# Feed-forward steps of 512 tokens by 128 inner units in place of 256 tokens by 256, in a fused attention and feed-forward kernel

## Chip, core and metric

The kernel runs on one core of one Trainium2 chip. The metric is the device time of one execution in microseconds (us). Besides plain executions there is one profiled execution with a trace of every engine: TensorE (PE, with its weight loads shown apart as PEld), VectorE (DVE), ScalarE (ACT), GpSimd (POOL), and SyncE (SP), which issues all DMAs here. Each engine works through its own queue strictly in order, and waits where an instruction's inputs or its buffer are not ready.

## What is computed

All data are float32; there are 4 batches, 8 heads, 768 positions, a head width of 64, and so 3072 tokens of width 512.

```python
# attention: a band of |i-j| < 16 in full, and 24 block summaries for the rest
k_sum = k.reshape(B, H, 24, 32, 64).max(axis=3)
v_sum = v.reshape(B, H, 24, 32, 64).mean(axis=3)
scores = concat([where(band, q @ k.T / 8, -1e9), q @ k_sum.T / 8 + log(32)])
a = softmax(scores)
x = (a @ concat([v, v_sum])).reshape(3072, 512)      # heads side by side
# feed-forward, w_in 512 x 2048, w_out 2048 x 512 (float64 in memory)
h = x @ w_in
g = h * tanh(softplus(h))                            # Mish
out = g @ w_out
```

## The kernel before

**Attention.** The 3072 tokens are 12 chunks of 256 (`NCH`, `CH`). A chunk is worked on in four units, one for each pair of heads (`HP`). A unit goes around all engines: `att_scores` (L240) does four score matmuls into one PSUM tile `sc` (L246; chunk 0 has smaller ones in L252 and L254), the mask and the row maximum on DVE (L261, four pairs of instructions), four exponentials on ACT (L266), the reciprocal of the sums on DVE (L269, L270), and the scaling on POOL (L271). `att_transpose` (L274) transposes on PE (`pt_ps`, L278) and copies on ACT (`pt`, L280). `att_values` (L283) multiplies by the values on PE (`x_ps`, L295); ACT rounds the result to `xh` (L296) and DVE takes the rest `xl` (L297). `sc`, `pt_ps` and `x_ps` share two PSUM buffers (`ps_a`; chunk 0 uses those of `ps_o`). The loads of a unit (`qk`, `vw`) have two buffers each.

**Precision.** Each feed-forward product is made of three matmuls, of a high and a low part: high by high, low by high, high by low.

**Weights.** 32 blocks of weights (16 of each matrix) come in as float64 and are turned into a high and a low part by `load_weight` (L107): per block four DVE instructions (L116, L117, L120, L122), two on ACT (L119, L124), one on POOL (L125). The loads go through three `stage` buffers, which the key and value summaries of batches 1 to 3 (`ks`, `vsum`) share.

**Feed-forward.** A step covers one chunk and 256 inner units. `ff_in` (L303) has 24 matmuls with 256 moving columns (L313) into `ph`, one PSUM bank of two (`ps_h`); `ff_act` (L317) is Mish on ACT (L321), the high part (L325, on ACT for chunks 0 and 1, else on DVE) and the low part on DVE (L326); `ff_out` (L329) has 12 matmuls with 512 columns (L340) into two banks `po`. There are 8 steps a chunk, 96 in all.

**Order.** The code before the main loop does chunk 0's attention and loads the first four weight blocks (L359). The main loop (L381) runs the steps of chunks 0 and 1 interleaved, and the others in order; `ff_out` follows two steps behind. The table `at` (L365 to L374) says at which step the parts of a unit are emitted, so that a chunk's four units are spread over the eight steps before it. Four, later two, weight blocks are loaded per step (L394). A scheduler then places the instructions on the engines' queues, so the emitted order is not quite the one that runs.

Of the kernel before, what the change touches and what calls it, by code (L numbers as in the profile page):

```python
# [55 lines left out]
def fused_kernel(ctx: ExitStack, tc: tile.TileContext, q0, qk, kt, v0, vw, vs, w_in, w_out, out):  # L56
# [49 lines left out]

    def load_weight(src, hi, lo, name):  # L107
        t = stage.tile([P, WP], I64, tag="stage", name=name)
        nc.sync.dma_start(t, src)
# [6 lines left out]
        nc.vector.tensor_scalar(out=x, in0=low, scalar1=29, scalar2=None, op0=ALU.logical_shift_right)  # L116
# [5 lines left out]
        nc.vector.scalar_tensor_tensor(out=u, in0=u, scalar=3, in1=x,  # L122
                                       op0=ALU.logical_shift_left, op1=ALU.bitwise_or)
        nc.scalar.copy(hi, f)  # L124
# [157 lines left out]

    def att_values(c, hp):  # L283
        u = units.pop((c, hp))
        if c not in xs:
            xs[c] = (xp.tile([P, HP, CH], F32R, tag="xh", name=f"xh{c}"),
                     xp.tile([P, HP, CH], F32R, tag="xl", name=f"xl{c}"))
        xh, xl = xs[c]
        ps = att_psum(c, f"x_ps{c}_{hp}")
        for s in range(NQ):  # L290
            for h in range(2):
                d = slice(h * D, (h + 1) * D)
# [2 lines left out]
                nc.tensor.matmul(x, u["v"][:, s, d], pt, start=True, stop=True)  # L295
# [7 lines left out]
    def ff_in(c, fp):  # L303
        i = c, fp
        xh, xl = xs[c]

        pool, tag = (ps_a, "a") if c == NCH - 1 and fp in (NP_ - 1, NP_ - 3) else (ps_h, "h")
        ph = pool.tile([P, 2, CH], F32, tag=tag, name=f"ph{c}_{fp}")
        for j in range(2):
            wh, wl = (weight(0, part, 2 * fp + j) for part in range(2))  # L310
            for cc in range(NCC):
                for n, (w, x) in enumerate(((wh, xh), (wh, xl), (wl, xh))):
                    nc.tensor.matmul(ph[:, j, :], w[:, cc * P:(cc + 1) * P], x[:, cc, :],  # L313
                                     start=(cc == 0 and n == 0), stop=(cc == NCC - 1 and n == 2))
        st[i] = {"h": ph.rearrange("p j t -> p (j t)")}

    def ff_act(c, fp):  # L317

        s = st[c, fp]
        g = ff.tile([P, 2 * CH], F32, tag="g", name=f"g{c}_{fp}", bufs=3)  # L320
        nc.scalar.activation(g, s["h"], AF.Mish)  # L321
        gh = ff.tile([P, 2 * CH], F32R, tag="gh", name=f"gh{c}_{fp}", bufs=3)
        gl = ff.tile([P, 2 * CH], F32R, tag="gl", name=f"gl{c}_{fp}", bufs=3)

        (nc.scalar.copy if c < 2 else nc.vector.tensor_copy)(gh, g)  # L325
        nc.vector.tensor_sub(gl, g, gh.bitcast(F32))  # L326
        s["g"] = (gh, gl)

    def ff_out(c, fp):  # L329
        i = c, fp  # L330
        gh, gl = st.pop(i)["g"]
        if fp == 0:
            po[c] = [ps_o.tile([P, DM], F32, tag="o", name=f"po{c}_{t}") for t in range(CH // P)]
        for t in range(CH // P):
            for j in range(2):
                fc = 2 * fp + j
                tok = slice(j * CH + t * P, j * CH + (t + 1) * P)
                wh, wl = (weight(1, part, fc) for part in range(2))
                for n, (g, w) in enumerate(((gh, wh), (gl, wh), (gh, wl))):
                    nc.tensor.matmul(po[c][t], g[:, tok], w,  # L340
                                     start=(fc == 0 and n == 0), stop=(fc == NFC - 1 and n == 2))
        if fp == NP_ - 1:
            for t in range(CH // P):
                o = ff.tile([P, DM], F32, tag="o", name=f"o{c}_{t}")
                nc.scalar.copy(o, po[c][t])
                nc.sync.dma_start(out[c * CH + t * P:c * CH + (t + 1) * P, :], o)
# [17 lines left out]
    start = 0  # L366
    for c in range(1, NCH):
        n = steps.index((c, 0)) - start
        for hp in range(HP):
            k = min(start + n - 3, start + n - 3 - 2 * (HP - 1 - hp) if c == 2 else start + n * hp // HP - 1)  # L370
            at.setdefault(max(k, 0), []).append((att_scores, c, hp))
            at.setdefault(max(k, 0) + 1, []).append((att_transpose, c, hp))
            at.setdefault(max(k, 0) + 2, []).append((att_values, c, hp))
        start += n  # L374
# [4 lines left out]

    loaded = HP + 1  # L380
    for i in range(len(steps) + 2):  # L381
        parts = at.get(i, ())
        now = [x for k, x in enumerate(steps) if turn(k, 0) == i]
        for x in now:
            ff_in(*x)
        for x in now:
            ff_act(*x)
# [56 lines left out]
```

## Time and profile before

| | us |
|---|---|
| median of 3 runs | 713.8 (709.15 to 714.37) |
| the profiled execution's own time | 712.24 |
| its span, from the first to the last instruction | 710.5 |
| PE busy | 672.8 (95%) |
| ACT busy | 354.2 (50%) |
| DVE busy | 301.1 (42%) |
| POOL busy | 111.5 (16%) |

Matmuls overlap, so PE's busy time says where PE has work, and not how fast it does it. Busy shares are averages over stages that differ: DVE is at 42% overall and close to full in the first quarter. A row of a timeline gives start, duration, engine, line, instruction, and in brackets how long the engine had been idle and what ended that. A row of the chain of waits gives start, duration and what was on the path that ended last. A row of a table of windows gives the stretch, its length, the busy time of each engine with its instructions in brackets, the clock granted to PE (1.00 is full), and the DMA engines' share and rate.

### The profile page before, as it was taken

How to read it: one execution, taken by the hardware profiler on the slowest of the kernel's cores; microseconds unless marked ns; L12 is line 12 of the kernel's file. 1: busy time of each engine (PE TensorE's matmuls, PEld its weight loads, DVE VectorE, ACT ScalarE, POOL GpSimd, SP SyncE). 2: the span in 40 equal slices, each digit the busy share in tenths (PEclk: the TensorE clock that was granted, in tenths of full speed). 3: DMA queues.
4: the chain of work that ended last, by engine and by line, in shares of the span. 5: the costliest groups of instructions: out<-in, count | busy, mean ns of one | idle time of the engine just before them, and what ended most of it. 6: DMA issues, size and time to landing. Idle time of an engine off the chain costs nothing.

```text
span 710.5 us, 12644 instructions
## 1 busy us (share of the span) xinstructions
PE 672.8 (95%) x4960; PEld 603.6 (85%) x4960; DVE 301.1 (42%) x872; ACT 354.2 (50%) x776; POOL 111.5 (16%) x151
## 2 busy tenths in 40 slices
PE   4978788799999999999999999999999999999998
PEld 3767677688898998998998998998998998998996
DVE  4899989952322334443223233222222322322211
ACT  2767755544556644644644644644644644644110
POOL 3454554301010010010100100100100100010000
PEclk9969899899999999999999999999999999999999
DMA  9876655772221323531311311311311311300000
GB/s 276 239 235 204 184 171 155 216 230 88 88 71 44 111 56 104 161 89 43 116 43 43 116 43 44 117 44 43 116 43 43 117 43 44 115 15 1 30 1 30
DMA packets 30683, 70.56 MB, mean 99 GB/s; under 512 B 4768, under 2 KB 9504, under 8 KB 30624
## 3 DMA queue, kind: packets, MB, share of 16 engines
q1 hardware_dynamic: 30624, 69.76, 32.2%
q8 instruction: 39, 0.64, 0.4%
q14 instruction: 20, 0.16, 0.1%
HBM read 61.15 MB, written 6.29 MB: 95 GB/s over the span
## 4 chain that ended last, share of the span: by engine, by line
PE 79%; DVE 11%; DMA 4%; issue 2%; ACT 2%; SPq 0%; POOL 0%; DVEq 0%; POOLq 0%
PE ph L313 34%; PE po L340 33%; PE sc L246 6%; PE x_ps L295 3%; DVE w_x L116 3%; PE pt_ps L278 2%; DVE w_x L117 2%; DVE w_f L122 2%; DMA ks<-kt 1%; DMA vsum<-vs 1%; DMA vw<-vw 1%; DVE w_f L120 1%; ACT pr L266 1%; DVE gl L326 1%; DVE vq L196 1%
## 5 line engine op out<-in xcount | busy, mean ns | idle before, releaser
L313 PE MATMUL ph<-xh,w_early_in_hi 128*128 128x256 f32 x480 | 138.7, 291 | 3.2 <-ACT w_early_in_hi L124 2.4
L313 PE MATMUL ph<-xh,w_early_in_lo 128*128 128x256 f32 x480 | 139.1, 291 | 2.2 <-POOL w_early_in_lo L125 2.2
L313 PE MATMUL ph<-xl,w_early_in_hi 128*128 128x256 f32 x480 | 138.9, 290 | 1.2 <-DVE xl L297 1.2
L325 DVE CAST gh<-g 128x512 fp32r<-128x512 f32 x80 | 34.3, 429 | 209.3 <-ACT g L321 196.6
L271 POOL TENSOR_TENSOR pr<-pr,rs 128x480 f32<-128x480 f32 x48 | 49.0, 1021 | 348.2 <-DVE rs L270 309.7
L313 PEld LDWEIGHTS ph<-xh,w_early_in_hi 128*128 128x128 f32 x480 | 93.9, 196 | 7.1 <-ACT w_early_in_hi L124 3.2
L313 PEld LDWEIGHTS ph<-xl,w_early_in_hi 128*128 128x128 f32 x480 | 93.8, 196 | 3.9 <-DVE xl L297 1.7
L313 PEld LDWEIGHTS ph<-xh,w_early_in_lo 128*128 128x128 f32 x480 | 93.9, 196 | 3.2 <-POOL w_early_in_lo L125 2.6
L340 PE MATMUL po<-w_early_out_hi,gh 128*128 128x512 f32 x240 | 94.3, 396 | 2.5 <-ACT gh L325 2.5
L340 PE MATMUL po<-w_early_out_hi,gl 128*128 128x512 f32 x240 | 95.6, 398 | 0.0
L340 PE MATMUL po<-w_early_out_lo,gh 128*128 128x512 f32 x240 | 95.0, 396 | 0.0
L321 ACT ACTIVATE g<-ph 128x512 f32<-128x512 f32 x96 | 57.4, 598 | 67.0 <-PE ph L313 66.5
L313 PE MATMUL ph<-xh,w_late_in_hi 128*128 128x256 f32 x288 | 82.5, 287 | 0.1
L313 PE MATMUL ph<-xh,w_late_in_lo 128*128 128x256 f32 x288 | 81.9, 284 | 0.1
L313 PE MATMUL ph<-xl,w_late_in_hi 128*128 128x256 f32 x288 | 81.1, 282 | 0.0
L266 ACT ACTIVATE pr<-pr,nm 128x120 f32<-128x120 f32 x192 | 73.7, 385 | 5.8 <-DVE nm L261 5.3
L321 ACT ACT_TABLE_LOAD x44 | 56.5, 1283 | 38.7 <-PE ph L313 38.3
L326 DVE TENSOR_TENSOR gl<-g,gh 128x512 fp32r<-128x512 f32 x96 | 70.7, 736 | 8.1 <-ACT gh L325 5.5
L296 ACT CAST xh<-x_ps 128x256 fp32r<-128x256 f32 x48 | 17.9, 372 | 100.7 <-PE x_ps L295 100.7
L280 ACT COPY pt<-pt_ps 120x512 f32<-120x512 f32 x48 | 28.1, 586 | 71.9 <-PE pt_ps L278 71.5
L266 ACT ACT_TABLE_LOAD x43 | 55.2, 1283 | 8.4 <-DVE nm L261 7.8
L340 PE MATMUL po<-w_late_out_hi,gl 128*128 128x512 f32 x144 | 56.7, 394 | 1.6 <-DVE gl L326 1.6
(75 smaller groups left out, 1149.9 us busy)
## 6 DMA issues: line engine op xcount, KB each, us to landing
qk<-qk SPq DMA_DIRECT2D x44, 496.0 KB
vw<-vw SPq DMA_DIRECT2D x48, 192.0 KB
w<-w_in SPq DMA_DIRECT2D x16, 512.0 KB
w<-w_out SPq DMA_DIRECT2D x16, 512.0 KB
ks<-kt SPq DMA_DIRECT2D x16, 384.0 KB
out<-o SPq DMA_DIRECT2D x24, 256.0 KB
vsum<-vs SPq DMA_DIRECT2D x12, 384.0 KB
vw<-vm SPq DMA_DIRECT2D x44, 48.0 KB
```

What stands on the lines that cost most here:

```text
L116: nc.vector.tensor_scalar(out=x, in0=low, scalar1=29, scalar2=None, op0=ALU.logical_shift_right)
L246: nc.tensor.matmul(ps[:, s * KA:(s + 1) * KA], u["qk"][:, s, 0:P], u["qk"][:, s, P:], start=True, stop=True)
L266: nc.scalar.activation(pr[:, s, :], pr[:, s, :], AF.Exp, scale=-1.0, bias=nm[:, s:s + 1], accum_out=sm[:, s:s + 1])
L271: nc.gpsimd.tensor_mul(pr, pr, rs.unsqueeze(2).broadcast_to([P, NQ, KA]))
L280: nc.scalar.copy(pt.rearrange("p s q -> p (s q)"), ps[:KA, :])
L295: nc.tensor.matmul(x, u["v"][:, s, d], pt, start=True, stop=True)
L296: nc.scalar.copy(xh[:, hp, :], ps[:, :CH])
L313: nc.tensor.matmul(ph[:, j, :], w[:, cc * P:(cc + 1) * P], x[:, cc, :], start=(cc == 0 and n == 0), stop=(cc == NCC - 1 and n == 2))
L321: nc.scalar.activation(g, s["h"], AF.Mish)
L325: (nc.scalar.copy if c < 2 else nc.vector.tensor_copy)(gh, g)
L326: nc.vector.tensor_sub(gl, g, gh.bitcast(F32))
L340: nc.tensor.matmul(po[c][t], g[:, tok], w, start=(fc == 0 and n == 0), stop=(fc == NFC - 1 and n == 2))
```

## The change

Two chunks form a group of 512 tokens (`CG`, `TG`, six groups `NG`). A step now covers one group and 128 inner units: `ff_in` has 12 matmuls of 512 columns, `ff_out` 12 as before, but into four `po` banks. There are 16 steps a group, and again 96. The attention of chunks 0 and 1 stands ahead of all steps, with six weight blocks among it; then each step loads two. The units of chunks 2 and 3 start at steps 6 to 13 of the first group; those of a later group at every second step of the group before. The steps run in plain order (`LEAD` and `AHEAD` are gone; so are the two last `ph` tiles in `ps_a`). `x` has two buffers of a group in place of three of a chunk. The tiles `f`, `x`, `a` (the Mish output) and `o` share one ring of six buffers. Of the four output copies of a group two go to DVE.

```diff
-NP_ = NFC // 2
+CG = 2
+TG = CG * CH
+NG = NCH // CG
-LEAD = 4
-AHEAD = 3
...
-    ff = ctx.enter_context(tc.tile_pool(name="ff", bufs=2))
+    ff = ctx.enter_context(tc.tile_pool(name="ff", bufs=6))
...
-        f = ff.tile([P, WP], F32, tag="f", name=f"{name}_f", bufs=3)
-        x = ff.tile([P, WP], U32, tag="x", name=f"{name}_x", bufs=2)
+        f = ff.tile([P, WP], F32, tag="t", name=f"{name}_f")
+        x = ff.tile([P, WP], F32, tag="t", name=f"{name}_x").bitcast(U32)
...
+    def ff_in(g, fc):
+        xh, xl = xs[g]
+        ph = ps_h.tile([P, TG], F32, tag="h", name=f"ph{g}_{fc}")
+        wh, wl = (weight(0, part, fc) for part in range(2))
+        for cc in range(NCC):
+            for n, (w, x) in enumerate(((wh, xh), (wh, xl), (wl, xh))):
+                nc.tensor.matmul(ph, w[:, cc * P:(cc + 1) * P], x[:, cc, :],
+                                 start=(cc == 0 and n == 0), stop=(cc == NCC - 1 and n == 2))
+        st[g, fc] = ph
...
+            if fc == NFC - 1:
+                o = ff.tile([P, DM], F32, tag="t", name=f"o{g}_{t}")
+                (nc.vector.tensor_copy if t % 2 else nc.scalar.copy)(o, po[g][t])
...
-    for what in "K0 K1 S0 W1 K2 V0 S1 W1 T0 K3 V1 S2 A0 T1 W1 V2 S3 A1 T2 V3 A2 T3 W1 L0 A3".split():
-        begins[what[0]](int(what[1:]))
+    begin_with("K0 K1 S0 K2 V0 S1 W1 T0 K3 V1 S2 A0 T1 V2 S3 W1 A1 T2 V3 A2 T3 l0 W1 A3")
     begin.close()
...
+    begin_with("l1 s0 W1 t0 s1 l2 a0 t1 s2 W1 l3 a1 t2 s3 W1 a2 t3 l4 a3")
...
+    for c, hp in todo[CG * HP:]:
+        g, half = divmod(c, CG)
+        u = half * HP + hp
+        k = NFC // 2 - 2 + u if g == 1 else (g - 1) * NFC + 2 * u - 1
...
-        load_weights(4 if i < LEAD else 2)
+        load_weights(2)
```

In the changed kernel the matmuls of `ff_in` are L310, Mish L317, the high and low part L321 and L322, the matmuls of `ff_out` L333; `x_ps` is L296, `xh` L297, `xl` L298. A number directly behind the letters of a name counts pairs of heads (`sc`, `pr`, `pt`, `x_ps`), steps (`ph`, `a`, `g`) or token blocks (`po`); `xh` and `xl` have none, and are whole chunks before, whole groups after. The last number is a running one.

The queue of PE where a chunk of the kernel before ends, around the value matmuls of the last unit of the next chunk (here the change from chunk 6 to 7 or one like it):

```order
L313 MATMUL ph_0_4047<-xh_3576,w_early_in_hi 128x256
L313 MATMUL ph_0_4047<-xl_3577,w_early_in_hi 128x256
L295 MATMUL x_ps_3_3998<-pt_3_3965,vw_3_3772 64x64 x8
L246 MATMUL sc_0_4009<-qk_0_3899 128x120 x4
L313 MATMUL ph_0_4047<-xh_3576,w_early_in_lo 128x256
L313 MATMUL ph_0_4047<-xh_3576,w_early_in_hi 128x256
L313 MATMUL ph_0_4047<-xl_3577,w_early_in_hi 128x256
L313 MATMUL ph_0_4047<-xh_3576,w_early_in_lo 128x256
L313 MATMUL ph_0_4047<-xh_3576,w_early_in_hi 128x256
L313 MATMUL ph_0_4047<-xl_3577,w_early_in_hi 128x256
L313 MATMUL ph_0_4047<-xh_3576,w_early_in_lo 128x256
L340 MATMUL po_0_3675<-w_late_out_hi,gh_6_3944 128x512
```

The same place in the changed kernel, where the second group ends. All the `ff_out` of that group stand ahead of these rows; behind them come the last six matmuls of `ph_0` and `ph_1`, and then the twelve of `ph_2`:

```order
L278 MATMUL pt_ps_2_2544<-ident,pr_2_2480 120x128 x4
L296 MATMUL x_ps_2_2570<-pt_2_2549,vw_2_2392 64x64 x8
L246 MATMUL sc_3_2581<-qk_3_2495 128x120 x4
L310 MATMUL ph_0_2747<-xh_1916,w_early_in_hi 128x512
L310 MATMUL ph_1_2785<-xh_1916,w_early_in_hi 128x512
L310 MATMUL ph_0_2747<-xl_1917,w_early_in_hi 128x512
L310 MATMUL ph_0_2747<-xh_1916,w_early_in_lo 128x512
L310 MATMUL ph_1_2785<-xl_1917,w_early_in_hi 128x512
L310 MATMUL ph_1_2785<-xh_1916,w_early_in_lo 128x512
L278 MATMUL pt_ps_3_2661<-ident,pr_3_2586 120x128 x4
L296 MATMUL x_ps_3_2687<-pt_3_2666,vw_3_2498 64x64 x8
L246 MATMUL sc_0_2698<-qk_0_2605 128x120 x4
```

Before, only the value part of the last unit and the scores of the next stand at the chunk's end, with `ff_in` and then 24 matmuls of `ff_out` behind them. Now the transposes of units 2 and 3, their value matmuls and two sets of scores follow one another there, with six matmuls of `ff_in` between the scores of unit 3 and its transposes, and none between a unit's transposes and its value matmuls.

The queue of ACT at that place in the changed kernel:

```order
L280 COPY pt_1_2443<-pt_ps_1_2438 120x512
L297 CAST xh_1916<-x_ps_1_2464 128x256
L266 ACT_TABLE_LOAD
L266 ACTIVATE pr_2_2480,sm_2_2486<-pr_2_2480,nm_2_2481 128x120 x4
L280 COPY pt_2_2549<-pt_ps_2_2544 120x512
L297 CAST xh_1916<-x_ps_2_2570 128x256
L266 ACTIVATE pr_3_2586,sm_3_2592<-pr_3_2586,nm_3_2587 128x120 x4
L280 COPY pt_3_2666<-pt_ps_3_2661 120x512
L297 CAST xh_1916<-x_ps_3_2687 128x256
L266 ACTIVATE pr_0_2703,sm_0_2709<-pr_0_2703,nm_0_2704 128x120 x4
L317 ACT_TABLE_LOAD
L317 ACTIVATE a_0_2760<-ph_0_2747 128x512
```

Before, a Mish stands between any two sets of exponentials; now three sets of exponentials stand in a row here, and the next group's first Mish is behind the third.

The queue of DVE in the first stage of the kernel before, while chunk 1's units 0 and 1 are at their maxima (`w_..` are instructions of weight blocks):

```order
L261 ISA pr_0_511,nm_0_512<-sc_0_506,base 128x120
L261 ISA nm_0_512 128x1
L116 TENSOR_SCALAR w_2_x<-w_2_580 128x512
L122 SCALAR_TENSOR_TENSOR w_3_f<-w_3_f,w_3_x 128x512
L120 TENSOR_SCALAR w_2_f<-w_2_f 128x512
L261 ISA pr_1_537,nm_1_538<-sc_1_532,base 128x120
```

And in the changed kernel the last block of the six that go with chunks 0 and 1, with chunk 1's first unit behind it:

```order
L117 SCALAR_TENSOR_TENSOR w_3_x<-w_3_627,w_3_x 128x512
L298 TENSOR_TENSOR xl_298<-x_ps_2_410,xh_297 128x256
L122 SCALAR_TENSOR_TENSOR w_3_f<-w_3_f,w_3_x 128x512
L298 TENSOR_TENSOR xl_298<-x_ps_3_445,xh_297 128x256
L261 ISA pr_0_475,nm_0_476<-sc_0_470,base 128x120
```

From there on DVE's queue holds only the parts of seven units (the four of chunk 1 and the first three of chunk 2), 73 rows in all, up to this place, where the other 26 weight blocks begin:

```order
L261 ISA pr_2_1173,nm_2_1174<-sc_2_1168,last 128x120
L261 ISA nm_2_1174 128x1
L116 TENSOR_SCALAR w_2_x<-w_2_692 128x512
L116 TENSOR_SCALAR w_4_x<-w_4_703 128x512
L117 SCALAR_TENSOR_TENSOR w_2_x<-w_2_692,w_2_x 128x512
```

Before, weight blocks and units alternate on DVE from the start; now there is a stretch of units alone, and the first step's Mish and the weights stand behind it.

More of the change, by code (lines that the diff above doesn't have):

```diff
@@ L130, in load_weights @@
         del weights[:n]
-    weights = [(w, 2 * fp + j) for fp in range(NP_) for w in range(2) for j in range(2)]
+    weights = [(0, 0)] + [(w, fc + 1 - w) for fc in range(NFC) for w in range(2) if fc + 1 - w < NFC]
     begin = ExitStack()
@@ L235, in att_psum @@
     def att_psum(c, name):
-        pool, tag = (ps_o, "o") if c == 0 else (ps_a, "a")
+        pool, tag = (ps_o, "o") if c < CG else (ps_a, "a")
         return pool.tile([P, 512], F32, tag=tag, name=name)
@@ L284, in att_values @@
         u = units.pop((c, hp))
[L285 to L288, printed above, removed]
+        g, half = divmod(c, CG)
+        if g not in xs:
+            xs[g] = (xp.tile([P, HP, TG], F32R, tag="xh", name=f"xh{g}"),
+                     xp.tile([P, HP, TG], F32R, tag="xl", name=f"xl{g}"))
+        xh, xl = (x[:, hp, half * CH:(half + 1) * CH] for x in xs[g])
         ps = att_psum(c, f"x_ps{c}_{hp}")
@@ L295, in att_values @@
                 nc.tensor.matmul(x, u["v"][:, s, d], pt, start=True, stop=True)
-        nc.scalar.copy(xh[:, hp, :], ps[:, :CH])
-        nc.vector.tensor_sub(xl[:, hp, :], ps[:, :CH], xh[:, hp, :].bitcast(F32))
+        nc.scalar.copy(xh, ps[:, :CH])
+        nc.vector.tensor_sub(xl, ps[:, :CH], xh.bitcast(F32))
     st = {}
     po = {}
[L303 to L346, printed above, removed]
@@ new lines, in ff_in, with ff_act @@
+    def ff_in(g, fc):
[7 more added lines that the diff above has]
+        st[g, fc] = ph
+    def ff_act(g, fc):
+        a = ff.tile([P, TG], F32, tag="t", name=f"a{g}_{fc}")
+        nc.scalar.activation(a, st[g, fc], AF.Mish)
+        ah = ff.tile([P, TG], F32R, tag="ah", name=f"ah{g}_{fc}", bufs=3)
+        al = ff.tile([P, TG], F32R, tag="al", name=f"al{g}_{fc}", bufs=3)
+        (nc.scalar.copy if g == 0 else nc.vector.tensor_copy)(ah, a)
+        nc.vector.tensor_sub(al, a, ah.bitcast(F32))
+        st[g, fc] = ah, al
@@ new lines, in ff_out @@
+    def ff_out(g, fc):
+        ah, al = st.pop((g, fc))
+        if fc == 0:
+            po[g] = [ps_o.tile([P, DM], F32, tag="o", name=f"po{g}_{t}") for t in range(TG // P)]
+        wh, wl = (weight(1, part, fc) for part in range(2))
+        for t in range(TG // P):
+            tok = slice(t * P, (t + 1) * P)
+            for n, (a, w) in enumerate(((ah, wh), (al, wh), (ah, wl))):
+                nc.tensor.matmul(po[g][t], a[:, tok], w,
+                                 start=(fc == 0 and n == 0), stop=(fc == NFC - 1 and n == 2))
+            if fc == NFC - 1:
+                o = ff.tile([P, DM], F32, tag="t", name=f"o{g}_{t}")
+                (nc.vector.tensor_copy if t % 2 else nc.scalar.copy)(o, po[g][t])
+                nc.sync.dma_start(out[g * TG + t * P:g * TG + (t + 1) * P, :], o)
@@ L349, in fused_kernel @@
     todo = [(c, hp) for c in range(NCH) for hp in range(HP)]
-    steps = [(c, i - c * LEAD) for i in range(NP_ + LEAD) for c in range(2) if 0 <= i - c * LEAD < NP_]
-    steps += [(c, fp) for c in range(2, NCH) for fp in range(NP_)]
+    steps = [(g, fc) for g in range(NG) for fc in range(NFC)]
     begins = {"K": lambda n: att_load_keys(0, n), "V": lambda n: att_load_values(0, n),
               "S": lambda n: att_scores(0, n), "T": lambda n: att_transpose(0, n),
-              "A": lambda n: att_values(0, n), "W": load_weights, "L": lambda n: att_load(1, n)}
@@ L359, in fused_kernel, with begin_with @@
-    for what in "K0 K1 S0 W1 K2 V0 S1 W1 T0 K3 V1 S2 A0 T1 W1 V2 S3 A1 T2 V3 A2 T3 W1 L0 A3".split():
-        begins[what[0]](int(what[1:]))
+              "A": lambda n: att_values(0, n), "W": load_weights, "l": lambda n: att_load(*todo[HP + n]),
+              "s": lambda n: att_scores(1, n), "t": lambda n: att_transpose(1, n),
+              "a": lambda n: att_values(1, n)}
+    def begin_with(parts):
+        for what in parts.split():
+            begins[what[0]](int(what[1:]))
+    begin_with("K0 K1 S0 K2 V0 S1 W1 T0 K3 V1 S2 A0 T1 V2 S3 W1 A1 T2 V3 A2 T3 l0 W1 A3")
@@ L361, in fused_kernel @@
     begin.close()
     late += weight_tiles(ctx.enter_context(tc.tile_pool(name="late", bufs=1)), "w_late", NFC - EARLY)
+    begin_with("l1 s0 W1 t0 s1 l2 a0 t1 s2 W1 l3 a1 t2 s3 W1 a2 t3 l4 a3")
     at = {}
[L366 to L374, printed above, removed]
@@ L376, in turn @@
-    def turn(k, lag):
-        return k + lag - (k >= len(steps) - AHEAD)
-    loaded = HP + 1
+    for c, hp in todo[CG * HP:]:
+        g, half = divmod(c, CG)
+        u = half * HP + hp
+        k = NFC // 2 - 2 + u if g == 1 else (g - 1) * NFC + 2 * u - 1
+        at.setdefault(k, []).append((att_scores, c, hp))
+        at.setdefault(k + 1, []).append((att_transpose, c, hp))
+        at.setdefault(k + 2, []).append((att_values, c, hp))
+    loaded = CG * HP + 1
     for i in range(len(steps) + 2):
@@ L382, in fused_kernel @@
         parts = at.get(i, ())
[L383 to L387, printed above, removed]
+        if i < len(steps):
+            ff_in(*steps[i])
+            ff_act(*steps[i])
         for f, c, hp in parts:
```

2 lines of the change are left out of this document (1 added, 1 removed).

## The prediction

> **What bounds the kernel now.** I read the profile's head and its table of windows first, to see where PE idles; then the chain of waits in the steady part, for what a step and a unit cost on PE; then the timelines of DVE, ACT and PE where the change rearranges work.
>
> ```profile
> span 710.5 us, 12644 instructions
> core 0: us, PE busy (x) PEld busy (x) DVE busy (x) ACT busy (x) POOL busy (x), PEclk, DMA share, GB/s
> 37.20:133.60 96.40, 81.59 (x534) 71.42 (x535) 93.80 (x182) 64.29 (x140) 46.94 (x38) 0.88 0.63 195
> 133.60:190.60 57.00, 50.03 (x338) 44.60 (x337) 26.72 (x67) 27.23 (x57) 6.49 (x8) 0.91 0.50 151
> 190.60:657.80 467.20, 467.20 (x3512) 423.06 (x3512) 147.38 (x540) 235.44 (x511) 43.25 (x68) 1.00 0.23 70
> ```
>
> Three stages with different limits. From 37.2 to 133.6, DVE is busy 93.8 of 96.4 us: it turns weights into high and low parts, and PE waits for them. Up to 190.6 PE catches up. Then PE never idles for 467.2 us, at full clock: there, time is what stands on PE's queue.
>
> ```profile
> 37.24 0.39 PE L313 MATMUL ph<-xh,w_early_in_hi 128*128 128x256 f32 x1 [1.13 <-ACT w_early_in_hi L124]
> 404.17 2.86 PE ph L313 x24
> 407.03 2.75 PE po L340 x12
> 411.10 0.44 PE pt_ps L278 x4
> 415.95 0.61 PE x_ps L295 x16
> 416.57 1.08 PE sc L246 x8
> 706.65 0.39 PE L340 MATMUL po<-w_late_out_lo,gh 128*128 128x512 f32 x1
> ```
>
> A 256-column matmul costs PE 2.86/24 = 0.119 us, a 512-column one 2.75/12 = 0.2296. A step is 5.61 us; a unit adds 0.44 + 0.61 + 1.08 = 2.13. From the first feed-forward matmul (37.24) to PE's end (707.04) are 669.8 us. The work in it is 2304 × 0.1192 + 1152 × 0.2296 + 44 units × 2.13 = 632.8; the other 37 us are waits and half clock, all before 190.6. The tail behind PE is 3.4 us. The profiled execution took 712.24, its span plus 1.7; the median, 713.8, is 0.2% above. I forecast in the span's frame and add 1.7.
>
> **The change part by part.** *Width.* Each two 256-column matmuls become one of 512. Nothing here shows an `ff_in` matmul of 512 columns; the `ff_out` ones have the same width and type, so I take 0.2296. The bounds are that and 2 × 0.1192. The gain is 1152 × (0.2384 − 0.2296) = 10.1 us; a step becomes 5.51.
>
> *The stretch of units alone.* Chunk 0's attention and the six blocks stay about where they were, so the stretch begins near 38.5. Then DVE's in-order queue has 73 rows of seven units and no weight row, and DVE is the engine that bounded this stage. How long does a unit take when nothing covers its chain?
>
> ```profile
> 402.07 1.15 PE L246 MATMUL sc<-qk 128*128 128x120 f32 x8
> 403.37 0.28 DVE L261 CUSTOM_DVE_ANT_0 pr<-sc,base 128x120 f32<-128x120 f32 x1 [0.35 <-PE sc L246]
> 403.88 0.40 ACT L266 ACTIVATE pr<-pr,nm 128x120 f32<-128x120 f32 x1
> 406.01 0.17 DVE L269 TENSOR_SCALAR rs<-sm 128x4 f32<-128x4 f32 x1 [1.74 <-ACT pr L266]
> 406.22 0.18 DVE L270 RECIPROCAL rs<-rs 128x4 f32<-128x4 f32 x1
> 407.34 0.99 POOL L271 TENSOR_TENSOR pr<-pr,rs 128x480 f32<-128x480 f32 x1
> 410.94 0.60 PE L278 MATMUL pt_ps<-ident,pr 128*120 128x128 f32 x4
> 411.57 0.59 ACT L280 COPY pt<-pt_ps 120x512 f32<-120x512 f32 x1 [2.57 <-PE pt_ps L278]
> 645.18 0.40 ACT L266 ACTIVATE pr<-pr,nm 128x120 f32<-128x120 f32 x1
> 646.62 0.19 ACT L266 ACTIVATION_READ_ACCUMULATOR pr<-pr,nm 128x1 f32 x1
> 647.21 1.28 ACT L321 ACT_TABLE_LOAD   x1 [0.41 <-PE ph L313]
> 648.51 0.60 ACT L321 ACTIVATE g<-ph 128x512 f32<-128x512 f32 x1
> ```
>
> From the scores to DVE 1.30 us, to ACT 0.51, four exponentials in a row 1.63 (645.18 to 646.81), the reciprocals 0.39, POOL 0.99, and about 0.2 for hand-offs: 5.0 us until the transposes can start. They take 0.44 before the next scores: 5.44 a unit if each waits for the last. Below, ACT alone needs 1.63 + 0.59 = 2.2. So seven units take 16 to 38 us. In PE's order, five score sets follow the transposes of the unit before or wait for a shared `ps_a` buffer, and two overlap with them: 5 × 5.44 = 27. PE is mostly idle there, and then its work takes longer:
>
> ```profile
> 40.95 1.90 PE L246 MATMUL sc<-qk 128*128 128x120 f32 x8
> ```
>
> 1.90 for the scores in place of 1.08, and the like for transposes: some 1.2 us a unit, 6 in all. I take **33**, near the upper bound. The 24 `ff_in` matmuls that stand among these rows lie in the waits.
>
> *The weights behind it.* 26 blocks are left.
>
> ```profile
> 103.75 1.51 DVE L116 TENSOR_SCALAR w_x<-w 128x512 uint32<-128x512 uint32 x1
> 109.71 1.51 DVE L116 TENSOR_SCALAR w_x<-w 128x512 uint32<-128x512 uint32 x1
> L116 DVE TENSOR_SCALAR w_x<-w x26: 392/1146/1526, 38.2 to 125.8; 128x512 uint32<-128x512 uint32 x26
> 131.07 0.27 DVE L261 CUSTOM_DVE_ANT_0 pr<-sc,base 128x120 f32<-128x120 f32 x1
> 131.87 0.68 DVE L326 TENSOR_TENSOR gl<-g,gh 128x512 fp32r<-128x512 f32 x1
> 133.60 0.67 DVE L122 SCALAR_TENSOR_TENSOR w_f<-w_f,w_x 128x512 uint32<-128x512 uint32 x1
> L326 DVE TENSOR_TENSOR gl<-g,gh 128x512 fp32r<-128x512 f32 x96 | 70.7, 736 | 8.1 <-ACT gh L325 5.5
> L172 DVE TENSOR_REDUCE km<-ks 128x24 f32<-128x768 f32 x16 | 15.1, 944 | 6.5 <-DMA ks<-kt 6.5
> L196 DVE TENSOR_REDUCE vq<-vsum 96x32 f32<-96x1024 f32 x12 | 14.6, 1212 | 10.3 <-DMA vsum<-vs 6.4 <-DMA vm<-vq 3.9
> ```
>
> Two blocks lie between 103.75 and 109.71: 2.98 us a block. Before, 26 blocks also came after 38.2, with units among them, and the last ended at 134.3. Now: 26 × 2.98 = 77.5; 14 low parts of the Mish output at 0.65 (0.736 less the overlap) = 9.1; three units at 1.6 (maxima 0.80, reciprocals 0.35, `xl` 0.42) = 4.8; five summaries of keys at 0.87 = 4.3, four of values at 1.25 = 5. Together 101 us: 38.5 + 33 + 101 = **172.5** for the last block, against 134.3. PE can't run ahead of it: 13 steps of 5.51 fit easily into 101 us.
>
> Behind the last block PE still has, up to the third step of the second group, 64 matmuls (14.7 us), attention pieces (7.0) and the end of the first group with its waits (4.3): **26**. By then 408 of 2304 feed-forward matmuls and 13 units are done, and one more unit's transposes and values are left over.
>
> *The steady part.* 1,896 matmuls × 0.2296 = 435.3, 31 units × 2.13 = 66.0, and 1.05: **502**.
>
> *The ends of groups.* The order shown for PE and ACT puts the chain of the last units bare on the path. Unit 3's transposes need 5.0 us from its scores, while scores and six matmuls are 1.08 + 1.38 = 2.46: a wait of 2.5. Twice, value matmuls stand right behind the transposes whose ACT copy they need: the copy ends 411.57 + 0.59 − 410.94 = 1.22 us after their start, against 0.44 of PE work: 0.8 each. Last, `ph_2` of the new group needs a `ps_h` buffer that `ph_0`'s Mish frees, and on ACT that stands behind the next unit's exponentials and a table load: 3.44 + 1.28 + 0.60 = 5.32 from those scores, against 2.46: 2.85. Sum 7.0. Of the four ends left, three cost 7.0 and the last 5.2, since no unit follows it: **26**. If other work covered these waits, nothing.
>
> After such a wait PE may run at half clock:
>
> ```profile
> 95.66 0.73 PE L340 MATMUL po<-w_early_out_hi,gh 128*128 128x512 f32 x2 [1.88 <-ACT gh L325]
> 97.00:98.00 1.00, 1.00 (x7) 1.00 (x7) 1.00 (x2) 0.92 (x3) 1.00 (x1) 0.52 0.84 332
> 99.00:100.00 1.00, 1.00 (x7) 1.00 (x6) 1.00 (x3) 0.65 (x2) 0.00 (x0) 0.50 0.00 0
> 101.00:102.00 1.00, 1.00 (x6) 0.83 (x5) 1.00 (x2) 0.00 (x0) 0.41 (x1) 1.00 0.60 160
> ```
>
> A gap of 1.88 us was followed by half clock until 101: about 5 us that lost 2.5. Four ends, each followed so, would lose 10, and none 0; from one place I can't tell how often, and take 1.5 each: **6**. [...]
>
> *The rest.* The shared ring of six buffers, the output copies on DVE and four `po` banks I cost at nothing: DVE is busy 147 of 467 us in the steady part and ACT 235, so they cover the extra rows; without that cover two copies of about 0.6 a group would be 7 us.
>
> **The sum.** 38.5 + 33 + 101 + 26 + 502 + 26 + 6 + 3.4 = 735.9 span, + 1.7 = **738 us**: 3.6% over the profiled 712.24, 3.4% over the median.
>
> **Rivals.** *A, faster: the ends of groups are hidden*, as ends of chunks are before, in the 467.2 us without idle. Then the 26 and the 6 go, and about 3 of the first group's end: 738 − 35 = 703. Against it stands the order: before, a Mish came between any two sets of exponentials, and 24 `ff_out` matmuls covered them. Chance 0.10.
>
> *B, no change: the stretch costs little.* If the units pipeline at ACT's 2.2 to 2.5 us, the stretch is 17 and not 33, and pieces of PE work run ahead in it: the last block comes near 150 and the time near 715. For it: two score sets do stand ahead. Against: two `ps_a` buffers and POOL in the chain. Chance 0.12.
>
> *C, slower still: the loads.* The eight summary tiles of batches 1 to 3 share three stage buffers with the weights, in SP's in-order queue. A load that waits for a buffer holds back those behind it, as here:
>
> ```profile
> 158.02 1.22 DVE L196 TENSOR_REDUCE vq<-vsum 96x32 f32<-96x1024 f32 x1 [3.69 <-DMA vsum<-vs]
> ```
>
> Before, such waits came when the weights were done; now some fall among them. Eight at about half of 3.69 are 14 us: 752. Chance 0.12.
>
> *D: the width brings nothing*, an `ff_in` matmul of 512 columns being no cheaper than two of 256: 738 + 10 = 748. Against it: the measured `ff_out` rows. Chance 0.04.
>
> **How the numbers follow.** The forecast has 0.62. Its own terms run from 16 to 38 in the stretch, 0 to 10 for the clock, some 8 either way for the weights: about 722 to 750. The range reaches to B and C: 712 to 756, which leaves A out. About 1% is what a measurement of this kernel can tell from no change, so 707 to 721 is "same". Faster: most of A, 0.09. Same: B and the edge of A, 0.13. Slower: the rest, 0.78.
>
> **What would show it.** In the changed profile: on DVE about 33 us from 38 with no weight row; the last L122 of the weights near 172; the twelve `ff_in` matmuls of the second group's third step near 198; `ff_in` steps of 2.75 and steps of 5.51; PE idle about 7 us at each of four group ends, ahead of L278, L296 and L310, with clock rows below 1.00 behind them; PE's last matmul near 732. A last block before 155 would refute the stretch, an idle-free steady part the group ends; steps of 5.6 the width. If weights waited for DMA for over 10 us, C holds.

## The result, and the profile after

The changed kernel takes 744.6 us (median of 4 runs, 742.62 to 746.26), the kernel before 714.1: a ratio of 1.043, with a 95% interval of 1.038 to 1.049. The forecast was 738, with a range of 712 to 756. The profiled execution took 742.62, its span is 740.9 against 735.9 in the sum.

The head of the page, and the table of windows, cut where the prediction cut its stages:

```profile
span 740.9 us, 10267 instructions
core 0: us, PE busy (x) PEld busy (x) DVE busy (x) ACT busy (x) POOL busy (x), PEclk, DMA share, GB/s
38.00:72.00 34.00, 21.69 (x173) 17.71 (x173) 11.23 (x70) 14.33 (x60) 9.42 (x14) 0.80 0.47 142
72.00:173.00 101.00, 87.18 (x403) 68.84 (x403) 92.60 (x172) 64.94 (x127) 48.26 (x32) 0.92 0.60 192
173.00:199.00 26.00, 24.46 (x174) 19.22 (x173) 11.48 (x41) 14.61 (x33) 5.60 (x7) 1.00 0.56 164
199.00:740.00 541.00, 514.83 (x2788) 417.41 (x2786) 160.73 (x534) 216.98 (x475) 40.93 (x62) 0.98 0.19 60
```

From 38 to 72 DVE is busy for 11.2 of 34 us, where the kernel before had it busy for 33.5; then it is busy for 92.6 of 101 us. And in the last row PE, which before was busy for all of the 516.4 us from 190.6 to 707, is busy for 515 of 541 us.

The stretch and the weights, from DVE's timeline (the first maximum of chunk 1's first unit, and the first weight row behind the units) and from the table of one source line (the last of 32 conversions starts at 171.6 and so ends at 172.3):

```profile
39.56 0.27 DVE L261 CUSTOM_DVE_ANT_0 pr<-sc,base 128x120 f32<-128x120 f32 x1
72.45 0.76 DVE L116 TENSOR_SCALAR w_x<-w 128x512 uint32<-128x512 uint32 x2
L122 DVE SCALAR_TENSOR_TENSOR w_f<-w_f,w_x x32: 674/680/1804, 17.0 to 171.6; 128x512 uint32<-128x512 uint32 x32
```

The end of a group on PE's timeline: the matmuls that waited when the second group ended (first four rows) and the third (last four), each with the wait and its releaser in brackets:

```profile
303.32 0.69 PE L296 MATMUL x_ps<-pt,vw 120*64 120x64 f32 x16 [0.68 <-ACT pt L280]
308.76 0.83 PE L278 MATMUL pt_ps<-ident,pr 128*120 128x128 f32 x4 [2.27 <-POOL pr L271]
310.27 1.12 PE L296 MATMUL x_ps<-pt,vw 120*64 120x64 f32 x16 [0.68 <-ACT pt L280]
317.45 0.51 PE L310 MATMUL ph<-xh,w_early_in_hi 128*128 128x512 f32 x1 [1.48 <-ACT a L317]
417.01 0.69 PE L296 MATMUL x_ps<-pt,vw 120*64 120x64 f32 x16 [0.68 <-ACT pt L280]
422.45 0.65 PE L278 MATMUL pt_ps<-ident,pr 128*120 128x128 f32 x4 [2.28 <-POOL pr L271]
423.78 0.69 PE L296 MATMUL x_ps<-pt,vw 120*64 120x64 f32 x16 [0.68 <-ACT pt L280]
429.56 0.50 PE L310 MATMUL ph<-xh,w_early_in_hi 128*128 128x512 f32 x1 [2.61 <-ACT a L317]
```

These are the four waits that were forecast, on the same matmuls and with the same releasers: the transposes for POOL's scaling, twice the values for ACT's copy, and `ph_2` for the Mish that frees its bank. And the granted clock (the number before the DMA share) at those two ends and the next:

```profile
309.00:315.00 6.00, 5.32 (x33) 4.42 (x32) 1.32 (x9) 2.10 (x8) 0.13 (x1) 0.51 0.25 68
418.00:424.00 6.00, 3.05 (x23) 2.20 (x24) 2.44 (x12) 2.33 (x10) 1.25 (x2) 1.00 0.42 128
424.00:430.00 6.00, 3.39 (x32) 2.67 (x29) 3.46 (x15) 4.37 (x13) 0.99 (x1) 1.00 0.50 158
534.00:541.00 7.00, 6.15 (x34) 5.01 (x34) 2.35 (x11) 2.54 (x9) 0.39 (x2) 0.53 0.27 77
```

A wait of 2.3 us is followed by over 6 us at half clock at 309 and 534, and by none at 423. What the traces show of that stands in the last experiment and the last section.

To compare stages I keep a book of PE for each kernel, since its work at full rate is known. Idle is the sum of the waits in PE's timeline (those above 0.15 us); half clock is the sum, over windows of 1 us, of PE's busy time times one minus the granted clock. All in us of the profiled execution:

| kernel | median | span | idle, 37 to 215 | half clock, 37 to 215 | idle, behind 215 | half clock, behind 215 |
|---|---|---|---|---|---|---|
| before | 714 | 710.5 | 22.7 | 14.7 | 0 | 0 |
| changed | 744.6 | 740.9 | 29.8 | 13.3 | 20.6 | 7.5 |
| rings apart | 753.8 | 750.3 | 35.5 | 16.1 | 19.9 | 9.3 |
| units early | 718.5 | 716.8 | 28.4 | 16.0 | 3.7 | 0 |
| two halves | 747.4 | 742.5 | 36.4 | 14.9 | 10.4 | 2.6 |
| rings apart, units early | 722.8 | 721.2 | 38.3 | 14.1 | 1.6 | 0 |
| chunks first, rings apart | 742.2 | 734.1 | 24.6 | 13.0 | 19.9 | 6.4 |
| the same, units early | 713.8 | 714.9 | 26.6 | 14.0 | 5.8 | 0 |
| chunks first, units early, shared ring | 704.0 | 702.4 | 23.7 | 10.9 | 0 | 0 |
| the same, two halves | 711.9 | 708.8 | 24.7 | 10.0 | 0 | 0 |

Between the first two rows lie 30.4 us of span: 28.1 at the ends of groups, 7.1 more idle and 1.4 less half clock in the first stage, 0.8 more in the tail behind PE (4.2 against 3.5), and 7.7 to 9.5 less for the width (measured further down). That makes 25 to 27. Each wait costs a little more than its brackets say: a matmul's row is 0.39 us long, while the next in a stream starts 0.23 behind its start, so by estimate some 0.16 is lost at every restart, 17 of them behind 215, 2.7 us. Some 1 to 3 us are not assigned.

### The profile page after: what moved, and what is told of

It reads as the page before. It is cut to its first block, busy times and chain, and to the rows that moved or that the text cites. A ratio compares the mean times of both kernels' runs of the same rounds, so it can differ in the third digit from the quotient of the medians.

```text
span 740.9 us, 10267 instructions
## 1 busy us (share of the span) xinstructions
PE 672.1 (91%) x3808; PEld 542.9 (73%) x3808; DVE 302.1 (41%) x884; ACT 332.3 (45%) x752; POOL 120.5 (16%) x151
## 3 DMA queue, kind: packets, MB, share of 16 engines
q1 hardware_dynamic: 30624, 69.76, 30.4%
## 4 chain that ended last, share of the span: by engine, by line
PE 70%; DVE 10%; ACT 8%; DMA 7%; issue 2%; POOL 2%; SPq 0%; POOLq 0%; DVEq 0%; ACTq 0%
PE po L333 30%; PE ph L310 28%; PE sc L246 6%; ACT pr L266 3%; PE x_ps L296 3%; PE pt_ps L278 3%; DMA w<-w_out 3%; DVE w_x L116 2%; DVE w_f L122 2%; DVE w_x L117 2%; ACT L317 1%; DMA ks<-kt 1%; DVE w_f L120 1%; DMA qk<-qk 1%; DMA v<-v 1%
## 5 line engine op out<-in xcount | busy, mean ns | idle before, releaser
L321 DVE CAST ah<-a 128x512 fp32r<-128x512 f32 x80 | 36.2, 453 | 212.5 <-ACT a L317 208.2
L317 ACT ACTIVATE a<-ph 128x512 f32<-128x512 f32 x96 | 57.3, 599 | 121.0 <-PE ph L310 117.3
L310 PE MATMUL ph<-xh,w_early_in_hi 128*128 128x512 f32 x240 | 96.8, 416 | 14.9 <-ACT a L317 10.9
L333 PE MATMUL po<-w_early_out_hi,al 128*128 128x512 f32 x240 | 95.6, 398 | 3.3 <-DVE al L322 3.3
L310 PE MATMUL ph<-xl,w_early_in_hi 128*128 128x512 f32 x240 | 97.3, 406 | 0.0
L310 PE MATMUL ph<-xh,w_early_in_lo 128*128 128x512 f32 x240 | 96.9, 404 | 0.0
L333 PE MATMUL po<-w_early_out_lo,ah 128*128 128x512 f32 x240 | 95.3, 397 | 0.0
L333 PE MATMUL po<-w_early_out_hi,ah 128*128 128x512 f32 x240 | 93.5, 398 | 0.3 <-ACT ah L321 0.3
L280 ACT COPY pt<-pt_ps 120x512 f32<-120x512 f32 x48 | 28.1, 585 | 99.3 <-PE pt_ps L278 99.3
L322 DVE TENSOR_TENSOR al<-a,ah 128x512 fp32r<-128x512 f32 x96 | 69.4, 725 | 6.7 <-ACT ah L321 4.2
L310 PEld LDWEIGHTS ph<-xh,w_early_in_hi 128*128 128x128 f32 x240 | 45.9, 197 | 27.8 <-ACT a L317 14.8
L298 DVE TENSOR_TENSOR xl<-x_ps,xh 128x256 fp32r<-128x256 f32 x48 | 20.2, 421 | 103.5 <-ACT xh L297 103.5
L297 ACT CAST xh<-x_ps 128x256 fp32r<-128x256 f32 x48 | 17.8, 371 | 93.8 <-PE x_ps L296 93.7
L333 PE MATMUL po<-w_late_out_hi,ah 128*128 128x512 f32 x144 | 56.9, 399 | 1.2 <-ACT ah L321 1.2
L333 PE MATMUL po<-w_late_out_hi,al 128*128 128x512 f32 x144 | 57.3, 398 | 0.2 <-DVE al L322 0.2
L310 PE MATMUL ph<-xh,w_late_in_lo 128*128 128x512 f32 x144 | 57.4, 399 | 0.0
L333 PE MATMUL po<-w_late_out_lo,ah 128*128 128x512 f32 x144 | 57.2, 397 | 0.0
L310 PE MATMUL ph<-xh,w_late_in_hi 128*128 128x512 f32 x144 | 57.2, 397 | 0.0
L310 PE MATMUL ph<-xl,w_late_in_hi 128*128 128x512 f32 x144 | 56.9, 395 | 0.0
```

What stands on the lines that cost most here:

```text
L280: nc.scalar.copy(pt.rearrange("p s q -> p (s q)"), ps[:KA, :])
L298: nc.vector.tensor_sub(xl, ps[:, :CH], xh.bitcast(F32))
L310: nc.tensor.matmul(ph, w[:, cc * P:(cc + 1) * P], x[:, cc, :], start=(cc == 0 and n == 0), stop=(cc == NCC - 1 and n == 2))
L317: nc.scalar.activation(a, st[g, fc], AF.Mish)
L321: (nc.scalar.copy if g == 0 else nc.vector.tensor_copy)(ah, a)
L322: nc.vector.tensor_sub(al, a, ah.bitcast(F32))
```

## The experiments

**Rings apart.** Is it the shared ring that empties DVE's queue of weights, and what is the emptied stretch worth? The weights' two scratch tiles get buffers of their own, out of the same six.

```diff
-    ff = ctx.enter_context(tc.tile_pool(name="ff", bufs=6))
+    ff = ctx.enter_context(tc.tile_pool(name="ff", bufs=2))
...
-        f = ff.tile([P, WP], F32, tag="t", name=f"{name}_f")
-        x = ff.tile([P, WP], F32, tag="t", name=f"{name}_x").bitcast(U32)
+        f = ff.tile([P, WP], F32, tag="f", name=f"{name}_f", bufs=2)
+        x = ff.tile([P, WP], F32, tag="x", name=f"{name}_x", bufs=2).bitcast(U32)
```

> The weights' f and x tiles get rings of two buffers each, and the Mish output and the output copies keep two: six in all, as before, but no longer one ring. In the order on DVE's queue the weight blocks then stand among the units from the start. Theory 1 (the stretch on DVE is made by the shared ring, since a weight block behind the first Mish output needs a buffer that this output frees, and it waits for chunk 1's attention): the 33 us stretch fills with blocks, the last weight conversion comes 18 to 25 us before the 172 us of the changed kernel, and the time falls from 744.6 to about 722. Theory 2 (the attention ahead of all steps is what costs, whatever DVE does in it): the last conversion moves by less than 5 us, and the time stays above 738. The group ends are as in the changed kernel by both.

The time is 753.8 us, 9 more than the changed kernel's. Neither theory had that. The table of L122 and the windows of this kernel:

```profile
L122 DVE SCALAR_TENSOR_TENSOR w_f<-w_f,w_x x32: 675/684/1795, 18.0 to 146.9; 128x512 uint32<-128x512 uint32 x32
38.00:72.00 34.00, 16.98 (x89) 13.88 (x86) 33.53 (x72) 17.61 (x47) 19.16 (x15) 0.55 0.64 210
```

The first half of theory 1 held: the stretch is full (DVE 33.5 of 34 us) and the last conversion comes 25 us earlier. The second half fell: that gains nothing. PE's timeline says why:

```profile
49.46 1.11 PE L278 MATMUL pt_ps<-ident,pr 128*120 128x128 f32 x4 [9.35 <-POOL pr L271]
57.18 1.22 PE L310 MATMUL ph<-xh,w_early_in_hi 128*128 128x512 f32 x2 [3.87 <-ACT xh L297]
98.76 0.80 PE L310 MATMUL ph<-xh,w_early_in_hi 128*128 128x512 f32 x1 [3.61 <-ACT a L317]
```

Now chunk 1's units queue behind weight blocks on DVE, ACT and POOL, and no step can be finished without all eight units of its 512 tokens. PE idles for 35.5 us in the first stage in place of 29.8, and half clock there takes 16.1 in place of 13.3. Weights and units are both needed before the steps can run, and the version with the units first is the shorter one. (The edit also leaves the Mish output and the output copies two buffers of their own, where they had drawn on six; what that alone costs was not tried.)

**Units early.** The ends of groups alone.

```diff
-        k = NFC // 2 - 2 + u if g == 1 else (g - 1) * NFC + 2 * u - 1
+        k = NFC // 2 - 2 + u if g == 1 else (g - 1) * NFC + 3 * u // 2 - 1
```

> The units of groups 3 to 6 start one and a half steps apart in place of two, so that the last value matmuls stand four matmul steps ahead of a group's end. Theory 1 (the bare chain of the last units at four group ends costs waits of 20.6 us by the profile, some 0.2 us more for each of 17 restarts, and 7.5 us of half clock behind them): all of it goes, 744.6 - 31 = 713. Theory 2 (the waits only move to other rows, since ACT's queue and two score buffers are the limit): 735 or more, with as much PE idle in the steady part. The first 200 us are as in the changed kernel by both.

718.5 us: 26 of the 31 us came back. Its window behind 215:

```profile
215.00:711.00 496.00, 492.30 (x2736) 402.32 (x2735) 151.67 (x511) 205.14 (x449) 38.71 (x59) 1.00 0.19 59
```

PE is at full clock throughout. The 3.7 us of waits that are left all lie in the second group (258 to 290 us), where the units now come closer together. The first stage is alike: 1.4 us less idle time and 2.7 more half clock. So the waits of a group's end did not move elsewhere; they were a matter of where the units stood.

**Two halves.** The width alone, in the changed kernel.

```diff
-        for cc in range(NCC):
-            for n, (w, x) in enumerate(((wh, xh), (wh, xl), (wl, xh))):
-                nc.tensor.matmul(ph, w[:, cc * P:(cc + 1) * P], x[:, cc, :],
+        for tok in (slice(0, CH), slice(CH, TG)):
+            for cc in range(NCC):
+                for n, (w, x) in enumerate(((wh, xh), (wh, xl), (wl, xh))):
+                    nc.tensor.matmul(ph[:, tok], w[:, cc * P:(cc + 1) * P], x[:, cc, tok],
```

> Only the width of the first product's matmuls is undone: each of 512 columns becomes two of 256, all else as in the changed kernel. Theory 1 (a matmul costs 0.2296 us at 512 columns and 0.1192 at 256): 948 pairs lie behind 202 us, at 8.8 ns each 8.3 us, and those before hide in waits for weights: 744.6 + 8 = 753. Theory 2 (the width changes nothing): within 2 us of 744.6.

747.4 us, 3 more, between the theories. It can't be read as the width's price: the scheduler placed the units otherwise with these instructions, so the ends cost 13.0 us in place of 28.1 and the first stage 8.2 more (the table). With these two, the 1.6 us by which the spans differ leave some 8.5 for the width. A later run repeats the edit where no wait can hide it.

**Both.** Rings apart, and units early.

> The first and the second edit together: rings apart, and units one and a half steps apart. Theory 1 (stretch and group ends are separate costs and add): 744.6 - 22 - 31 = 692, faster than the kernel before by 3%. Theory 2 (one of the two hides behind the other, or PE's own work is the limit near the time before): 710 or more.

722.8 us. Theory 1's 692 is out, since the 22 us that it took for the rings had not come in the first experiment either. The units early are worth 31 us with rings apart as well (753.8 to 722.8), so this part adds. Against units early with the shared ring (718.5) it is 4 us more, but the runs of the two overlap (717.6 to 721.9 and 718.9 to 727.9), so that this difference is not clear of the noise.

**Chunks first.** The first group alone is worked as before: steps of 256 tokens and 256 inner units, chunk 1's attention among chunk 0's steps. `chunk_in`, `chunk_act` and `chunk_out` are the step of the kernel before.

```diff
+    begin_with("K0 K1 S0 W1 K2 V0 S1 W1 T0 K3 V1 S2 A0 T1 W1 V2 S3 A1 T2 V3 A2 T3 W1 l0 A3")
...
-    steps = [(g, fc) for g in range(NG) for fc in range(NFC)]
+    steps = [(chunk_in, chunk_act, chunk_out, c, i - c * LEAD)
+             for i in range(NP_ + LEAD) for c in range(CG) if 0 <= i - c * LEAD < NP_]
+    steps += [(ff_in, ff_act, ff_out, g, fc) for g in range(1, NG) for fc in range(NFC)]
```

> The first group alone is worked as in the kernel before: steps of one chunk and 256 inner units, those of chunks 0 and 1 interleaved, chunk 1's attention among chunk 0's steps, weights in that order. Rings apart as in the first experiment; groups 2 to 6 and their ends as in the changed kernel. To 202 us the changed kernel has 44.5 us in which PE isn't doing full-rate work, the kernel before 37. Theory 1 (in the first stage the change costs only the difference, 7.5 us, since DVE's conversions hold PE up there with either order): 744.6 - 7.5 = 737, and 753.8 - 16 = 738 seen from the first experiment. Theory 2 (the attention ahead of all steps costs the whole stretch of 33 us): about 712.

742.2 us with rings apart, 11.5 less than the first experiment's 753.8, which differs from it in the first group alone. In the book the first stage loses 37.6 us in place of 51.6, as in the kernel before (37.4). Theory 2, 712, is out; theory 1 was 5 us low.

**Chunks first, units early.**

> The same, with the units of groups 3 to 6 one and a half steps apart as in the second experiment. Theory 1 (first stage as before, no waits at group ends, and 960 pairs of matmuls at 8.8 ns each saved): 713.7 - 8.4 = 705, faster than the kernel before. Theory 2 (the wide steps gain nothing by themselves): 712 to 716.

713.8 us, with a wide spread (709.6 to 717.7). That is inside theory 2's numbers, but not for theory 2's reason: 5.8 us of idle time stand behind 215, all in the second group, again at its units. The next run has none.

**The same with the shared ring.**

> The same as the run before it but with the one shared ring of six buffers for weights, Mish output and output copies. On DVE's queue chunk 1's units then precede the seventh weight block. Theory 1 (the first experiment's lesson holds: units first or weights first is nearly a draw, since both are needed): within 6 us of the run before it. Theory 2 (the shared ring is a cost of its own): 10 to 20 us slower.

704.0 us: 10 faster than its neighbour, where I had expected as good or slower, and 1.2% faster than the kernel before (ratio 0.988, interval 0.983 to 0.992). Its windows:

```profile
37.00:215.00 178.00, 154.26 (x1062) 131.04 (x1063) 127.31 (x308) 120.00 (x266) 64.35 (x57) 0.92 0.56 178
215.00:697.00 482.00, 482.00 (x2658) 394.39 (x2657) 146.28 (x494) 198.57 (x435) 35.59 (x57) 1.00 0.19 58
```

Behind 215 PE is never idle. On DVE the maxima of three of chunk 1's units now come ahead of the fifth weight block (the last of them from 40.15), and those of the fourth stand behind the seventh's first row. With rings apart they come between 37.4 and 67.5, the first behind six blocks and the last behind fourteen. (In these kernels L118 begins a block, and L263 is a maximum.)

```profile
43.52 1.48 DVE L118 TENSOR_SCALAR w_x<-w 128x512 uint32<-128x512 uint32 x3
47.06 0.27 DVE L263 CUSTOM_DVE_ANT_0 pr<-sc,base 128x120 f32<-128x120 f32 x1
```

So the shared ring is better in two of three pairs: by 9 us in the changed kernel (744.6 against 753.8) and by 10 here; with units early (718.5 against 722.8) the difference lies inside the spread. The two spans here differ by 12.5 us; the book has 6.0 more in the first stage, 5.8 behind 215, and the tail behind PE is 1.5 longer (5.7 against 4.2). How much of it is the order on DVE and how much the two buffers that Mish output and output copies have with rings apart, these runs don't separate. Against the second experiment (718.5), which has the same ring and the same ends, working the first group by chunks is worth 14.4 us.

**The width where nothing hides it.** The edit of the two halves, in this kernel.

> The fastest kernel so far (first group by chunks, units one and a half steps apart, shared ring; 704.0) with the width alone undone in groups 2 to 6: each matmul of 512 columns in the first product becomes two of 256. In it PE has no idle time after 215 us, so that a price of the width can't hide in waits or change a group's end. Theory 1 (0.2384 against 0.2296 us a pair, 960 pairs): 704.0 + 8.4 = 712. Theory 2 (the third experiment's 3 us is all that the width is worth): 705 to 708.

711.9 us: 7.9 more, the span 6.4. Its chain, and behind it that of the kernel with whole steps:

```profile
403.88 2.88 PE ph L313 x24
```

```profile
401.85 2.73 PE ph L312 x12
```

The first stage is alike in both (34.8 and 34.6 us lost), neither idles behind 215, and the matmuls of one `ff_in` differ by 0.15 us in these rows. Theory 1 holds: 960 pairs at 6.7 to 8.2 ns are the gain of the width.

With this run three edits stand on top of one another: units early took away 26.1 us, working the first group by chunks 14.4, and matmuls of 256 columns added 7.9. They lead from 744.6 to 711.9, and the kernel before takes 714, so that little else of the change is left to explain.

**The clock alone.**

> This kernel leaves out the whole computation: 42 bursts of 72 matmuls of 512 columns, 16.5 us each, with ACT copies of the result between them, one to seven in turn, six times each, so that PE idles about 0.9 to 4.5 us between bursts. Theory 1 (whether a gap is followed by half clock depends on its length alone): one length from which on all six gaps are followed by it, and none below. Theory 2 (a gap counts by how it falls into windows that run on regardless): at middle lengths, 1.5 to 3 us, some of the six are and some are not, the share rising with length. [...]

It was executed once (885.5 us). Gaps of one length, and how many were followed by half clock:

| idle time of PE | 0.69 | 1.34 | 1.99 | 2.63 | 3.28 | 3.93 | 4.58 |
|---|---|---|---|---|---|---|---|
| followed by half clock | 0 of 6 | 0 of 6 | 3 of 6 | 6 of 6 | 6 of 6 | 6 of 6 | 5 of 5 |

Two gaps of the same length on PE's timeline, each with two windows of 3.41 us (this kernel has no DVE column, and PEclk is the third number from the end):

```profile
60.88 1.65 PE L32 MATMUL ps<-x,w 128*128 128x512 f32 x3 [1.99 <-ACT x L39]
57.47:60.89 3.42, 1.43 (x8) 0.86 (x6) 1.83 (x3) 0.00 (x0) 1.00 0.00 0
60.89:64.30 3.41, 3.41 (x8) 2.73 (x9) 0.00 (x0) 0.00 (x0) 0.50 0.00 0
```

```profile
204.63 1.66 PE L32 MATMUL ps<-x,w 128*128 128x512 f32 x6 [1.99 <-ACT x L39]
200.83:204.25 3.42, 1.81 (x9) 1.16 (x7) 1.50 (x3) 0.00 (x0) 1.00 0.00 0
204.25:207.66 3.41, 3.03 (x13) 2.54 (x14) 0.33 (x1) 0.00 (x0) 1.00 0.03 5
```

The length alone does not decide at 1.99 us, so theory 1 is out, and the counts are what theory 2 asks for. As long as bursts follow, the stretches at half clock in this run are 3.41 or 6.83 us long, and their starts lie whole numbers of 3.41 us apart: 60.89, 81.37 and 101.85 are 20.48 us, six times 3.41, behind one another. The windows above are cut at such places. The gap before 60.88 lies whole in the window from 57.47, where PE is busy for 1.43 us, and the next window runs at half clock. The gap before 204.63 is cut by a border into 1.61 and 0.38 us, and no half clock follows. These two gaps are 143.75 us apart, 42.1 times 3.41; if the other repeats of a length follow at about that distance, as I estimate from these two, the six are not six independent cases. "6 of 6" thus does not say that every gap of 2.63 us is followed by half clock.

## Why the prediction came out right, step by step

- **The stretch of units alone.** Forecast 33 us from 38.5; measured 32.9 (39.56 to 72.45). The count of the units was right: of the six intervals between their maxima one is overlapped (0.81 us), and five are 5.39 to 7.07 us long. What made them longer than 5.44 was not mainly half clock (below the list), so that the 33 is in part luck.
- **The last conversion.** Forecast 172.5, measured 172.3. The 101 us from the stretch to there were summed as work of DVE alone. Measured were 99.9, of which DVE worked 91.5 and waited about 8, 6.5 of them for ACT. The work was put too high, the waits were left out, and the two cancel.
- **What the stretch is worth.** The sum took the last conversion as the gate of the first stage, and that was wrong as a cause: with rings apart the gate opened 25 us earlier and the time rose by 9. Eight units must also be through before any step of 512 tokens can be finished. The sum came out because it followed the one order that this kernel has. Rival B fell twice: its stretch of 17 us did not come, and with rings apart the last block at 147.6 did not bring the time near 715 either.
- **The shared ring "at nothing".** It was no cost, but not for the reason given. It is what sorts DVE's queue into units first and weights behind (all of chunk 1's units in the changed kernel, three of four in the fastest), and without it the time is 9 and 10 us longer in two pairs of runs, and not clearly longer in the third.
- **Behind the last block.** Forecast 26 us to the third step of the second group; measured 29.7 (172.3 to 201.99). Its last wait, for the Mish, is 2.28 us, and two waits for `ah` and `al` of 1.18 and 0.23 were not in the sum.
- **The ends of groups.** Forecast 26 us over four ends; measured 20.6 in the brackets, about 23 with the restarts. The transposes waited for 2.27 to 2.33 (forecast 2.5), the values twice for 0.68 at most (0.8); the Mish wait was 1.48, 2.61, 1.87 in two parts, and none at the last end (2.85). That units placed earlier bring 26 us back shows the cause, and rival A, the ends hidden, is out.
- **Half clock.** Forecast 6 us, measured 7.5, at three of four ends: two windows of 3.41 us at two of them, one at the third. The third group's end, with waits of 2.28 and 2.61 us, lost none, so that by estimate the four ends could as well have lost more or less. The row of 1.88 us had been misread, too: half clock behind it lasted from 97.04 to 100.45, 3.41 us at a clock of 0.50, which cost 1.7 us and not 2.5.
- **The steady part.** Steps at 2.73 to 2.75 us each half, as forecast. From the third step of the second group to PE's end are 534.7 us, where the sum has 502 + 26 + 6 = 534.
- **The width.** Forecast 10.1 us for 1152 pairs, 8.8 ns each; measured 6.7 to 8.2 ns, which makes 7.7 to 9.5 us. Rival D is out.
- **The loads (rival C).** Of DVE's waits between 72.45 and 172.3, 1.5 us were for loads of weights, and none for a summary. Rival C asked for over 10.
- **What the sum missed.** The span was 740.9 against 735.9. Of these 5 us, 3.7 lie behind the last block, 1.1 before the stretch, 0.7 in the steady part with its ends and 0.8 in the tail, and the stretch and the weights give back 1.3.

In the stretch of units the sum put 6 us of half clock on top of the chain. But PE ran at full clock for 20 of the 33 us, with the two longest intervals among them. In the longest (51.33 to 58.40), matmuls of `ff_in`, which the sum had taken to lie in the waits, stand ahead of the next scores on PE's queue, and those scores then waited for POOL, which copies the key summaries into their tile. Nor was PE mostly idle: it was busy for 21.1 of the 32.9 us.

```profile
46.28:66.76 20.48, 13.01 (x117) 9.92 (x114) 6.52 (x49) 9.32 (x41) 5.16 (x9) 1.00 0.53 161
55.76 1.15 PE L246 MATMUL sc<-qk 128*128 128x120 f32 x8 [1.28 <-POOL qk L212]
```

Where the 30 us come from is thus not what the longest term of the sum suggests. The stretch of 33 us is the most visible thing in the profile, but the first stage lost only 43.1 us of PE against 37.4 before. The ends of groups, which look small, are 28.1. (Working the first group by chunks gained 14.4 us, more than this difference of 5.7: the first stage of the fastest kernel loses 34.6, less than before, and the 3.7 us of waits in the second group go as well.)

## What to carry to other kernels

A stage that looks empty on one engine is worth what the same stage loses in the other version, not its length: keep a book of the bound engine's idle and throttled time by stage, for both kernels. When work is regrouped into fewer, larger steps, look at the last items of the previous group's hidden work: a chain around four engines needs independent matmuls between its links, and moving it a few steps ahead of the boundary brought back 26 of 30 us here. A width that saves 8 ns a pair is worth having only when the regrouping that it asks for is free: the version with both, 704.0 us, keeps the small steps where they let work start early.
